# Pooled attention and a squared-ReLU network: pooling by accumulating transfers, a longer lag of the second product, and SyncE's transfers in another order

## The chip, the cores and the metric

The kernel runs on one core of one Trainium2 chip. The metric is the device time of one execution in microseconds (us). Engines are called as the profile calls them: PE (matrix product; PEld is its loading of weights), DVE (vector), ACT (scalar), POOL (GpSimd), SP (SyncE, which issues transfers), and a "q" behind a name means the engine's instruction queue. Differences of about 0.5% are the least that runs of this kernel can tell from nothing.

## The reference, cut to what matters

```python
def _attn_ref(q, k, v):                        # each 8 x 8 x 576 x 64: batch, head, token, width
    k_p = k.reshape(B, H, 72, 8, D).mean(axis=3)   # every 8 tokens of keys become one
    v_p = v.reshape(B, H, 72, 8, D).mean(axis=3)
    scores = scale * np.matmul(q, k_p.transpose(0, 1, 3, 2))
    scores = scores - np.max(scores, axis=-1, keepdims=True)
    attn = np.exp(scores)
    attn = attn / (np.sum(attn, axis=-1, keepdims=True) + 1e-09)
    return np.matmul(attn, v_p)

x = attn_out.transpose(0, 2, 1, 3).reshape(4608, 512)
h = np.maximum(x @ w_in, 0.0)                  # w_in 512 x 2048
return h * h @ w_out                           # w_out 2048 x 512
```

The two weights come as 64-bit floats and are turned into 32-bit floats on the chip.

## The kernel before, in words

The 4608 tokens go through in nine chunks of 512 (`CH`, numbered 0 to 8). A chunk has 16 steps, one for each block `fc` of 128 hidden units, so there are 144 steps; the loop over them is at line 734. In step s, PE makes the first product (x times w_in, tile `h`) of step s, and then the second product (squared ReLU times w_out, tiles `o`, function `project`) of step s - LAG, with LAG = 2. What the attention needs is woven into the same steps.

**The first product.** From chunk 2 on the function `seven` makes two blocks `fc` at once with seven products in place of eight: 24 matmuls in an even step, 18 in an odd one, each 128x256. Sums of quarters of x and of the weights (`x_sums`, `x_operand`; `sum_of_quarters`) feed it, and DVE and ACT add the parts up in PSUM (tiles `u` and `h`: `soon` in the even step). In the odd step, `activate` makes r = relu(h) and its square on ACT, for both blocks.

**High and low parts.** Products at nearly full precision are made of three: each operand is split into a rounded high part and what is left. ACT copies the high part, DVE subtracts: `gh` and `gl` from r (`split_hidden`, line 564), `x_B`/`x_T` from sums of x, `st` from q, `kh`/`kl` from pooled keys. `project` is 12 matmuls of 128x512 in a step: for each of four `o` tiles two with `gh` and one with `gl`.

**w_out.** Its 16 blocks, split, are kept in device memory (`kept`), and each block is fetched again for each chunk (`fetch_weights`, line 200): a transfer of 512 KB, issued from ACT's queue, one step ahead of its use (STREAM = 1). It lands in one of the 39 slots of 4 KB per partition that all large tiles share (`w_tile`, SLOTS).

**Keys and values.** Those of batches 0 and 1 are pooled at the start, by additions on POOL. From batch 2 on, `kv_steps` (line 702) plans, for each of the 8 heads, a load of 72 rows of 8 x 64 numbers (`load_head`, 144 KB, from SP) and two steps later one reduction on DVE (`pool_head`, line 243): tiles `kq` for keys, `vp` for values. The table KV_AT holds the steps, counted from KV0 = -37 before the chunk that first needs the batch: k in the steps 0 to 9, PE's transposition `turn_k` (tile `kps`) in step 13, v in the steps 18 to 31. Six batches (2 to 7) go this way, one for each of the chunks 2 to 7.

**Attention of a chunk.** For each of four pairs of heads, from chunk 2 on, eight stages follow at the distances in `STEADY` from the steps -23, -19, -15 and -11 before the chunk: q is loaded (two steps ahead, QL) and transposed on DVE; `scores` on PE (tiles `sps`), then a maximum over partitions on POOL (tile `mx`, PARTITION_ALL_REDUCE); `exponents` two steps later, with a sum over partitions on POOL (`tot`); `send_sums` and `fetch_sums` carry the sums through device memory (`rs`, `rc`) to another layout, `reciprocals` works on them on DVE (`rr`) and sends them (`rd`), `fetch_reciprocals` spreads them over partitions (`rb`); `weigh_values` is PE's product with the values (`av`), which DVE multiplies by `rb` into `xf`. Chunks 0 and 1 have stages of their own (`token_...`).

**What sets the order.** No scheduler moves anything: the class `InOrder` (line 26) keeps every instruction, on its engine, in the order in which the loop writes it down, and each engine works strictly in that order. A tile tag with `bufs` buffers makes an instruction wait until the tile that lay there has been read. SP, ACT's queue and POOL are such orders too: a transfer that waits holds up all transfers behind it.

Of the kernel before, what the change touches and what calls it, by code (L numbers as in the profile page):

```python
# [9 lines left out]
F32 = mybir.dt.float32  # L10
# [27 lines left out]
def pooled_attn_relu2_ffn(  # L38
# [42 lines left out]


    STEADY = ((-23, -19, -15, -11), (0, 1, 3, 5, 5, 6, 6, 8))
    KV0 = -37
    EARLY = ((-16, -13, -10, -8), (0, 1, 2, 3, 4))
    KV_AT = ((0, 1, 2, 3, 4, 5, 8, 9), 13, (18, 19, 22, 23, 26, 27, 30, 31))
# [15 lines left out]
    def load(dst, src):  # L102
        loads.append((dst, src))
# [77 lines left out]
    def sum_of_quarters(g, name):  # L181
        (e, kh), a, b, op = {"S1": ((1, 1), (1, 0), (1, 1), ALU.add), "S3": ((1, 0), (0, 0), (1, 0), ALU.subtract),
                             "S2": ((1, 1), (1, 1), (0, 0), ALU.subtract), "S4": ((0, 1), (0, 1), (1, 1), ALU.subtract)}[name]
        t = quarter(g, e, kh)
        DVE.tensor_tensor(t, quarter(g, *a), quarter(g, *b), op=op)
        split_operand(g, name, t)

    stored = {}

# [23 lines left out]
    def load_head(kind, b, h):  # L213
        t = loaded[kind, b, h] = sb.tile([SP_, POOL * D], F32, name=f"{kind}_{b}_{h}", tag="ld", bufs=LD)
        load(t, {"k": k, "v": v}[kind][b, h].rearrange("(s o) d -> s (o d)", o=POOL))

    def load_pair(kind, b, p):
        t = loaded[kind, b, p] = w_tile(F32, f"{kind}8_{b}_{p}")[:SP_]
# [8 lines left out]
        GP.tensor_tensor(dst, src[:, :, :D], src[:, :, D:2 * D], op=ALU.add)  # L227

    def halve_k(b, p):
        kp = loaded["kp", b, p] = sb.tile([SP_, 2, D], F32, name=f"kq_{b}_{p}", tag="kq", bufs=4)  # L230
        by_halves(kp, loaded.pop(("k", b, p)))

    def halve_v(b, p):
# [6 lines left out]
        for i in range(2):  # L240
            DVE.tensor_reduce(kv[b][:, 2 * p + i, :], t[:, i].rearrange("p (o d) -> p d o", d=D), axis=AX.X, op=ALU.add)

    def pool_head(kind, b, h):
        new_batch(b)
        if kind == "v":
            dst = kv[b][:, h, :]
        else:
            if h % 2 == 0:
                loaded["kp", b, h // 2] = sb.tile([SP_, 2, D], F32, name=f"kq_{b}_{h // 2}", tag="kq", bufs=4)
            dst = loaded["kp", b, h // 2][:, h % 2, :]  # L250
        DVE.tensor_reduce(dst, loaded.pop((kind, b, h)).rearrange("p (o d) -> p d o", d=D), axis=AX.X, op=ALU.add)

    def turn_k(b, pairs=range(NPAIR)):

# [84 lines left out]
        return then  # L339

    def reduced(kind, c, p):
        return [sb.tile([SP_, CH], F32, name=f"{kind}_{c}_{p}_{i}", tag="mx", bufs=4) for i in range(2)]

    def exponents(c, p):
        sc, mx = live.pop((c, p))
# [96 lines left out]

    def weigh_values(c, p):

        if c >= PLAIN and p == 0:
            xf[c] = sb.tile([P, NPAIR, CH], F32, name=f"xf_{c}", tag="xf", bufs=1)
        sc, rb = live.pop((c, p))
        av = (ps_a if c else ps_h).tile([P, 512], F32, name=f"av_{c}_{p}", tag="a" if c else "h")
        for b, o, n in segments(c):
            for i in range(2):  # L450
                PE.matmul(av[i * D:(i + 1) * D, o:o + n], lhsT=kv[b][:, 2 * p + i, :], rhs=sc[:, i, o:o + n],
                          start=True, stop=True)

        def then():
            if c == 0:
                x = xts[c, p] = x_tile(F32, f"x_{c}_{p}")
                ACT.copy(x[:, 0, :], av)
            elif c < PLAIN:
                x = xts[c, p] = x_tile(F32R, f"x_{c}_{p}")
                split(x[:, 0, :], x[:, 1, :], av)  # L460
            else:
                DVE.tensor_tensor(xf[c][:, p, :], av, rb, op=ALU.mult)

        return then

# [1 line left out]

    def x_sums(c):

        one, two = (xf[c][:, i:i + 2, :].rearrange("p c (h t) -> p h c t", h=2) for i in (0, 2))  # L470
# [4 lines left out]
    minus = {"T2": "T1", "T4": "T2"}  # L475

    def x_operand(c, name):
        src = xf[c][:, :2, :HT] if name == "B11" else parts[name]
# [65 lines left out]
    def hidden(c, fc):  # L544
        if c < PLAIN:
            hps = [(fc, plain(c, fc))]
        else:
            hps = seven(c, fc)
            if fc % 2 == 0:
                return hps  # L550

        def activate():
            for f, hp in hps:
                if c == 0:
                    r = gts[c, f] = sb.tile([P, CH], F32, name=f"r_{c}_{f}", tag="gl" if f % 2 else "gh", bufs=2)
                else:
                    r = gts[c, f] = sb.tile([P, CH], F32, name=f"r_{c}_{f}", tag="r", bufs=2)
                ACT.activation(r, hp, AF.Relu)
            for f, _ in hps:
                ACT.activation(gts[c, f], gts[c, f], AF.Square)  # L560

        return (activate, None, None) if c >= PLAIN else (None, None, activate)

    def split_hidden(c, fc):
        if c == 0:
            return
        gh = sb.tile([P, CH], F32R, name=f"gh_{c}_{fc}", tag="gh", bufs=2)
# [109 lines left out]
        halve_k(1, p)  # L677
    for p in range(NPAIR):
        halve_v(1, p)
    at(0, turn_k, 1)  # L680
    at(9, split_k, 1)


# [16 lines left out]
            at(c * NFC + i + LAG - STREAM, fetch_weights, c, i)  # L700

    def kv_steps(b, s):
        k_at, turn_at, v_at = KV_AT
        for h in range(H):
            at(s + k_at[h], load_head, "k", b, h)
            at(s + k_at[h] + 2, pool_head, "k", b, h)
            at(s + v_at[h], load_head, "v", b, h)
            at(s + v_at[h] + 2, pool_head, "v", b, h)
        at(s + turn_at, turn_k, b)
# [90 lines left out]
```

## Time and profile before

| what | value |
|---|---|
| median of 3 runs | 1018.83 us (1016.66 to 1021.34) |
| profiled execution | 1017.44 us |
| its span, first to last instruction | 1015.5 us, so 1.94 us lie around it |
| mean granted clock of PE | 0.978 |
| PE busy | 937.0 us (92%) |
| DVE busy | 651.0 us (64%) |
| ACT busy | 513.6 us (51%) |
| POOL busy | 335.1 us (33%) |

A page of the profile lists, for each engine, the busy time and groups of instructions: output tile <- input tiles, the shape, how many (x), busy us in all, mean ns of one, and how long the engine stood idle just before them, with who ended it. The view of windows gives the same by stretches of time, the view of waits who waited for whom, and the timeline single instructions. Matmuls overlap, so a PE that reads as busy can still be slowed down; how far apart they start tells more.

### The profile page before, as it was taken

The numbers are of one execution on the slowest core, as the hardware profiler recorded it, in microseconds if no ns is written. First come the engines' busy times: TensorE is split into PE (matmuls) and PEld (weight loads), VectorE is DVE, ScalarE is ACT, GpSimd is POOL, SyncE is SP. The second block draws the span as 40 slices with busy tenths as digits, with TensorE's granted clock in tenths as the row PEclk, the third lists the DMA queues.
The fourth block names the chain that finished last, engine by engine and source line by source line (L and its number), as shares of the span: only waits on it lengthen the run. The fifth ranks groups of instructions, "written<-read, shape, count | busy, mean of one in ns | idle before, by whom it ended". The sixth has DMA issues, their size and how long they took to land.

```text
span 1015.5 us, 14298 instructions
## 1 busy us (share of the span) xinstructions
PE 937.0 (92%) x5050; PEld 728.1 (72%) x5050; DVE 651.0 (64%) x1043; ACT 513.6 (51%) x1015; POOL 335.1 (33%) x162
## 2 busy tenths in 40 slices
PE   5789999998988989999999998999999999999997
PEld 3334444576866777787878786878788878888996
DVE  4877288867577777866686658665856675434231
ACT  2565476555555454644455535544554465435333
POOL 6720013443415434343444432433344434300000
PEclk9989999999999999999999899999999999999999
DMA  9667404475433433543445344543344434223223
GB/s 222 189 164 238 135 0 138 154 252 189 152 86 132 124 116 109 170 143 111 122 140 169 117 123 119 169 122 117 116 157 117 114 107 160 95 105 135 103 104 125
DMA packets 133686, 138.65 MB, mean 137 GB/s; under 512 B 91576, under 2 KB 91576, under 8 KB 133616
## 3 DMA queue, kind: packets, MB, share of 16 engines
q1 hardware_dynamic: 115184, 70.63, 24.6%
q10 hardware_dynamic: 18432, 67.12, 19.3%
q8 instruction: 40, 0.66, 0.3%
q14 instruction: 30, 0.25, 0.1%
HBM read 119.65 MB, written 18.06 MB: 136 GB/s over the span
## 4 chain that ended last, share of the span: by engine, by line
PE 54%; DVE 23%; ACT 9%; DMA 7%; issue 4%; SPq 2%; POOL 1%; ACTq 0%; DVEq 0%; POOLq 0%
PE o L34 26%; PE h L34 24%; DVE gl L34 4%; DMA w_o<-kept 4%; DVE h L34 3%; DVE vp L34 2%; SPq L34 2%; PE sps L34 2%; DVE xf L34 2%; DVE kq L34 2%; ACT sc L34 2%; PE av L34 2%; DMA k<-in_k_dram 1%; DVE sc L34 1%; DVE st L34 1%
## 5 line engine op out<-in xcount | busy, mean ns | idle before, releaser
L34 PE MATMUL o<-w_o,gh 128*128 128x512 f32 x1024 | 331.5, 405 | 23.0 <-ACT gh L34 15.1
L34 POOL PARTITION_ALL_REDUCE tot<-sc x56 | 183.0, 3315 | 327.6 <-ACT sc L34 238.2
L34 PEld LDWEIGHTS o<-w_o,gh 128*128 128x128 f32 x1024 | 188.5, 193 | 71.8 <-ACT gh L34 23.2
L34 PE MATMUL o<-w_o,gl 128*128 128x512 f32 x512 | 209.1, 408 | 18.6 <-DVE gl L34 17.6
L34 POOL PARTITION_ALL_REDUCE mx<-sc x56 | 111.9, 2046 | 207.1 <-ACT sc L34 177.9
L34 DVE TENSOR_TENSOR gl<-r,gh 128x512 fp32r<-128x512 f32 x128 | 114.6, 895 | 93.5 <-ACT gh L34 92.7
L34 ACT ACTIVATE r<-h 128x512 f32<-128x512 f32 x144 | 85.8, 596 | 111.7 <-PE h L34 71.3
L34 PEld LDWEIGHTS o<-w_o,gl 128*128 128x128 f32 x512 | 98.5, 192 | 57.4 <-DVE gl L34 37.1
L34 PE MATMUL h<-x_T,w_S 128*128 128x256 f32 x1008 | 131.4, 284 | 2.2 <-DVE x_T L34 1.4
L34 PEld LDWEIGHTS h<-x_T,w_S 128*128 128x128 f32 x1008 | 125.1, 192 | 3.8 <-DVE x_T L34 2.2
L34 ACT COPY u<-h 128x256 f32<-128x256 f32 x112 | 41.8, 373 | 131.3 <-DVE h L34 67.1
L34 DVE TENSOR_TENSOR h<-h,u 128x256 f32<-128x256 f32 x168 | 72.6, 432 | 50.9 <-ACT u L34 26.8
L34 PE MATMUL h<-x_B,w_A 128*128 128x256 f32 x672 | 99.4, 284 | 0.0
L34 PEld LDWEIGHTS h<-x_B,w_A 128*128 128x128 f32 x672 | 93.4, 193 | 4.8
L34 ACT ACTIVATE r<-r 128x512 f32<-128x512 f32 x144 | 84.2, 625 | 1.0
L34 ACT CAST gh<-r 128x512 fp32r<-128x512 f32 x128 | 78.5, 613 | 1.6 <-PE o L34 0.4
L34 ACT ACTIVATE sc<-sc 72x512 f32<-72x512 f32 x56 | 34.5, 632 | 68.3 <-DVE sc L34 68.3
L34 PE MATMUL o<-wf_o,r 128*128 128x512 f32 x128 | 61.6, 627 | 0.0
L34 PE MATMUL h<-x,wf_i 128*128 128x512 f32 x128 | 61.4, 625 | 0.0
L34 DVE TENSOR_TENSOR st<-qs,st 64x512 fp32r<-64x512 f32 x56 | 42.1, 751 | 27.1 <-ACT st L34 26.3
L34 DVE TENSOR_TENSOR u<-h,u 128x256 f32<-128x256 f32 x56 | 23.6, 421 | 53.9 <-ACT u L34 53.4
L34 DVE TENSOR_REDUCE kq<-k 72x64 f32<-72x512 f32 x48 | 50.7, 1060 | 7.1 <-PE kps L34 6.2
(85 smaller groups left out, 1179.3 us busy)
## 6 DMA issues: line engine op xcount, KB each, us to landing
w_o<-kept ACTq DMA_DIRECT2D x128, 512.0 KB
out_dram<-ob SPq DMA_DIRECT2D x36, 256.0 KB
raw_i<-in_moe_w_in_dram SPq DMA_DIRECT2D x16, 512.0 KB
raw_o<-in_moe_w_out_dram SPq DMA_DIRECT2D x16, 512.0 KB
kept<-w_o SPq DMA_DIRECT2D x16, 512.0 KB
rb<-rd SPq DMA_DIRECT2D x56, 128.0 KB
k<-in_k_dram SPq DMA_DIRECT2D x48, 144.0 KB
v<-in_v_dram SPq DMA_DIRECT2D x48, 144.0 KB
```

The lines of the kernel that those rows point to most:

```text
L34: return lambda *a, **k: self.tc.keep_in_program_order(f(*a, **k))
```

## The change

1. **Pooling.** `load_head` and `pool_head` go. `load_sums` brings the keys of a batch as four rounds of [72 partitions, 8 heads, 2 x 64 numbers]: round 0 is a plain load from SP, and the rounds 1 to 3 are added onto it in the same tile by transfers that accumulate, issued from POOL, two (four heads each) for a round. `pool` then makes one addition on DVE of the two halves, for all 8 heads. The same for values. The tile `two` has one buffer, so each of these steps waits for the one before it.
2. **Steps of it.** KV_AT becomes (k from step 3, v from step 9), KV0 becomes -34: for keys, rounds in the steps 3 to 6, the addition in 8, `turn_k` in 9; for values, rounds in 9 to 12, the addition in 14.
3. **The lag.** LAG becomes 3: `project` in step s is for step s - 3. `split_hidden` stays at s - 2, so `gh` and `gl` are written a step before they are used; they get three buffers each.
4. **Subtractions held back.** The DVE half of a split goes on a list `behind` and is written down by `catch_up`: in odd steps before `soon`, in all steps after PE's part.
5. **SP.** `fetch_weights` moves from ACT's queue to SP's, to the start of a step (still one step ahead of use). `fetch_sums` and `fetch_reciprocals` come next, ahead of the loads, one step later than before (`STEADY` (0, 1, 3, 5, 5, 6, 6, 8) becomes (0, 1, 3, 5, 6, 6, 7, 8)); `x_sums` moves to the end of a step.
6. **Room.** SLOTS 40 for 39; `xf` becomes two of these slots; tag `ld` two buffers for three, `mx` three for four, `kq` one of eight heads for four of two.

On PE, the rows below are the end of the first product in an odd step and the start of the second product behind it, in chunk 2 (`h_10`, `h_11` are the blocks of the step pair; the digit behind `w_o`, `gh` and `gl` is the block `fc` that is projected). Before:

```order
L34 MATMUL h_10_3006<-x_B_2210,w_S_2795 128x256 x6
L34 MATMUL h_10_3006<-x_B_2283,w_A_1653 128x256 x6
L34 MATMUL h_11_3007<-x_T_2287,w_A_1773 128x256 x6
L34 MATMUL o_0_2478<-w_o_9_3073,gh_9_3104 128x512 x2
L34 MATMUL o_0_2478<-w_o_9_3073,gl_9_3105 128x512
```

The same place now:

```order
L34 MATMUL h_10_2911<-x_B_2131,w_S_2738 128x256 x6
L34 MATMUL h_10_2911<-x_B_2198,w_A_1592 128x256 x6
L34 MATMUL h_11_2912<-x_T_2202,w_A_1731 128x256 x6
L34 MATMUL o_0_2447<-w_o_8_2949,gh_8_2951 128x512 x2
L34 MATMUL o_0_2447<-w_o_8_2949,gl_8_2952 128x512
```

Behind the same products of block 11 stands block 8 of the second product, where block 9 stood.

On POOL, the rows below run from the sums of one pair of heads to the maxima of the next chunk's first pair (ISA rows with `mx` are maxima, with `tot` sums; the digit behind them is the pair). Before:

```order
L34 ISA mx_2_0_2499<-sc_2_2498 72x512
L34 ISA mx_2_1_2500<-sc_2_2498 72x512
L34 ISA tot_2_0_2642<-sc_2_2498 72x512
L34 ISA tot_2_1_2643<-sc_2_2498 72x512
L34 ISA mx_3_0_2776<-sc_3_2775 72x512
L34 ISA mx_3_1_2777<-sc_3_2775 72x512
L34 ISA tot_3_0_2935<-sc_3_2775 72x512
L34 ISA tot_3_1_2936<-sc_3_2775 72x512
L34 ISA mx_0_0_3065<-sc_0_3064 72x512
L34 ISA mx_0_1_3066<-sc_0_3064 72x512
L34 ISA tot_0_0_3203<-sc_0_3064 72x512
```

The same place now, with batch 4's keys and values:

```order
L34 ISA mx_2_0_2396<-sc_2_2395 72x512
L34 ISA mx_2_1_2397<-sc_2_2395 72x512
L34 DMA k_4_2326<-in_k_dram 72x4x128 x6
L34 ISA tot_2_0_2554<-sc_2_2395 72x512
L34 ISA tot_2_1_2555<-sc_2_2395 72x512
L34 ISA mx_3_0_2680<-sc_3_2679 72x512
L34 ISA mx_3_1_2681<-sc_3_2679 72x512
L34 DMA v_4_2760<-in_v_dram 72x4x128 x2
L34 ISA tot_3_0_2842<-sc_3_2679 72x512
L34 ISA tot_3_1_2843<-sc_3_2679 72x512
L34 DMA v_4_2760<-in_v_dram 72x4x128 x2
L34 ISA mx_0_0_2971<-sc_0_2970 72x512
```

Six accumulating transfers (three rounds) stand between the maxima and the sums of pair 2; the rounds for values stand one by one between later reductions, the third behind the rows shown.

The diff, cut to its core:

```diff
-    LAG, QL = 2, 2
+    LAG, QL = 3, 2
-    SLOTS, STREAM, LD = 39, 1, 3
+    SLOTS, STREAM, LD = 40, 1, 2
-    STEADY = ((-23, -19, -15, -11), (0, 1, 3, 5, 5, 6, 6, 8))
-    KV0 = -37
+    STEADY = ((-23, -19, -15, -11), (0, 1, 3, 5, 6, 6, 7, 8))
+    KV0 = -34
...
+    behind = []
+
+    def catch_up():
+        while behind:
+            behind.pop(0)()
+
     def split_operand(g, name, src):
         t = wt[g, name] = w_tile(F32R, f"w_{g}_{name}")
-        split(in_blocks(t[:, 0, :]), in_blocks(t[:, 1, :]), src)
+        hi, lo = in_blocks(t[:, 0, :]), in_blocks(t[:, 1, :])
+        ACT.copy(hi, src)
+        behind.append(lambda: DVE.tensor_tensor(lo, src, hi.bitcast(F32), op=ALU.subtract))
...
     def fetch_weights(c, fc):
         t = wt["o", fc] = w_tile(F32R, f"w_o_{c}_{fc}")
-        ACT.dma_start(t.bitcast(F32), stored[fc])
+        dma(t.bitcast(F32), stored[fc])
...
-    def pool_head(kind, b, h):
-        new_batch(b)
+    two = {}
+
+    def load_sums(kind, b, j):
+
+        if j == 0:
+            new_batch(b)
+            two[kind] = sb.tile([SP_, H, 2 * D], F32, name=f"{kind}2_{b}", tag="two", bufs=1)
+        src = {"k": k, "v": v}[kind][b].rearrange("h (s j o) d -> j s h (o d)", j=POOL // 2, o=2)[j]
+        if j == 0:
+            load(two[kind], src)
+        else:
+            for n in range(0, H, H // 2):
+                GP.dma_start(two[kind][:, n:n + H // 2], src[:, n:n + H // 2], accum_op=ALU.add)
+
+    def pool(kind, b):
+        t = two.pop(kind)
...
-        DVE.tensor_reduce(dst, loaded.pop((kind, b, h)).rearrange("p (o d) -> p d o", d=D), axis=AX.X, op=ALU.add)
+        DVE.tensor_tensor(dst, t[:, :, :D], t[:, :, D:], op=ALU.add)
...
-        gh = sb.tile([P, CH], F32R, name=f"gh_{c}_{fc}", tag="gh", bufs=2)
-        gl = sb.tile([P, CH], F32R, name=f"gl_{c}_{fc}", tag="gl", bufs=2)
-        split(gh, gl, gts[c, fc])
+        gh = sb.tile([P, CH], F32R, name=f"gh_{c}_{fc}", tag="gh", bufs=3)
+        gl = sb.tile([P, CH], F32R, name=f"gl_{c}_{fc}", tag="gl", bufs=3)
+        r = gts[c, fc]
         gts[c, fc] = (gh, gl)
+        ACT.copy(gh, r)
+        behind.append(lambda: DVE.tensor_tensor(gl, r, gh.bitcast(F32), op=ALU.subtract))
...
+        for kind, start in KV_AT:
+            for j in range(POOL // 2):
+                at(s + start + j, load_sums, kind, b, j)
+            at(s + start + POOL // 2 + 1, pool, kind, b)
+        at(s + KV_AT[0][1] + POOL // 2 + 2, turn_k, b)
...
-        if 0 <= s - LAG < len(steps):
-            split_hidden(*steps[s - LAG])
+        for f, a in todo:
+            if f is fetch_weights:
+                f(*a)
+        if 0 <= s - 2 < len(steps):
+            split_hidden(*steps[s - 2])
         if store:
             store()
         store = project(*steps[s - LAG]) if s >= LAG else None
+        if s % 2:
+            catch_up()
         if soon:
             soon()
         for f in later:
             f()
         if then:
             then()
+        catch_up()
+        first = (load_q, load_sums)
         for f, a in todo:
-            if f is fetch_weights:
+            if f in (fetch_sums, fetch_reciprocals):
+                f(*a)
+        for f, a in todo:
+            if f in first:
                 f(*a)
         issue_loads()
         for f, a in todo:
-            if f is not fetch_weights and f not in on_pe + last + (x_operand,):
+            if f not in first + on_pe + last + (x_sums, x_operand, fetch_weights, fetch_sums, fetch_reciprocals):
                 f(*a)
```

More of the change, by code (lines that the diff above doesn't have):

```diff
@@ L71, in pooled_attn_relu2_ffn @@
     SCALE = 1.0 / (D ** 0.5) / POOL
[L72 removed]
+    LAG, QL = 3, 2
     PLAIN = 2
     SQ = 32
[L76 removed]
+    SLOTS, STREAM, LD = 40, 1, 2
     FIRST, EAGER, AHEAD = 2, 8, 3
     PRO, RATE, MARGIN = 5, 2, 1
[L83 to L86 removed]
+    STEADY = ((-23, -19, -15, -11), (0, 1, 3, 5, 6, 6, 7, 8))
+    KV0 = -34
+    EARLY = ((-15, -12, -10, -7), (0, 1, 2, 3, 4))
+    KV_AT = (("k", 3), ("v", 9))
     X_AT = (("B11", -9), ("B22", -2), ("T1", -2), ("T3", -2), ("T2", -1), ("B21", -1), ("T4", -1))
@@ L185, in sum_of_quarters @@
         DVE.tensor_tensor(t, quarter(g, *a), quarter(g, *b), op=op)
-        split_operand(g, name, t)
+        behind.append(lambda: split_operand(g, name, t))
     stored = {}
@@ L211, in pooled_attn_relu2_ffn @@
     heads = [(i, slice(i * D, (i + 1) * D), slice((1 - i) * D, (2 - i) * D)) for i in range(2)]
-    def load_head(kind, b, h):
-        t = loaded[kind, b, h] = sb.tile([SP_, POOL * D], F32, name=f"{kind}_{b}_{h}", tag="ld", bufs=LD)
-        load(t, {"k": k, "v": v}[kind][b, h].rearrange("(s o) d -> s (o d)", o=POOL))
     def load_pair(kind, b, p):
@@ L229, in halve_k @@
     def halve_k(b, p):
-        kp = loaded["kp", b, p] = sb.tile([SP_, 2, D], F32, name=f"kq_{b}_{p}", tag="kq", bufs=4)
+        if p == 0:
+            loaded["kq", b] = sb.tile([SP_, H, D], F32, name=f"kq_{b}", tag="kq", bufs=1)
+        kp = loaded["kp", b, p] = loaded["kq", b][:, 2 * p:2 * p + 2, :]
         by_halves(kp, loaded.pop(("k", b, p)))
@@ L241, in reduce_v @@
             DVE.tensor_reduce(kv[b][:, 2 * p + i, :], t[:, i].rearrange("p (o d) -> p d o", d=D), axis=AX.X, op=ALU.add)
-    def pool_head(kind, b, h):
-        new_batch(b)
+    two = {}
[11 more added lines that the diff above has]
+        t = two.pop(kind)
         if kind == "v":
-            dst = kv[b][:, h, :]
+            dst = kv[b]
         else:
-            if h % 2 == 0:
-                loaded["kp", b, h // 2] = sb.tile([SP_, 2, D], F32, name=f"kq_{b}_{h // 2}", tag="kq", bufs=4)
-            dst = loaded["kp", b, h // 2][:, h % 2, :]
-        DVE.tensor_reduce(dst, loaded.pop((kind, b, h)).rearrange("p (o d) -> p d o", d=D), axis=AX.X, op=ALU.add)
+            dst = sb.tile([SP_, H, D], F32, name=f"kq_{b}", tag="kq", bufs=1)
+            for p in range(NPAIR):
+                loaded["kp", b, p] = dst[:, 2 * p:2 * p + 2, :]
+        DVE.tensor_tensor(dst, t[:, :, :D], t[:, :, D:], op=ALU.add)
     def turn_k(b, pairs=range(NPAIR)):
@@ L341, in reduced @@
     def reduced(kind, c, p):
-        return [sb.tile([SP_, CH], F32, name=f"{kind}_{c}_{p}_{i}", tag="mx", bufs=4) for i in range(2)]
+        return [sb.tile([SP_, CH], F32, name=f"{kind}_{c}_{p}_{i}", tag="mx", bufs=3) for i in range(2)]
     def exponents(c, p):
@@ L443, in weigh_values @@
     def weigh_values(c, p):
-        if c >= PLAIN and p == 0:
-            xf[c] = sb.tile([P, NPAIR, CH], F32, name=f"xf_{c}", tag="xf", bufs=1)
+        if c >= PLAIN and p % 2 == 0:
+            xf[c, p // 2] = w_tile(F32, f"xf_{c}_{p // 2}")
         sc, rb = live.pop((c, p))
@@ L461, in then @@
             else:
-                DVE.tensor_tensor(xf[c][:, p, :], av, rb, op=ALU.mult)
+                DVE.tensor_tensor(xf[c, p // 2][:, p % 2, :], av, rb, op=ALU.mult)
         return then
@@ L468, in x_sums @@
     def x_sums(c):
-        one, two = (xf[c][:, i:i + 2, :].rearrange("p c (h t) -> p h c t", h=2) for i in (0, 2))
+        one, two = (xf[c, i].rearrange("p c (h t) -> p h c t", h=2) for i in range(2))
         parts.update({"B11": one[:, 0], "B21": two[:, 0], "B22": two[:, 1], "T1": one[:, 0], "T3": one[:, 1], "T2": two[:, 1], "T4": two[:, 0]})
@@ L477, in x_operand @@
     def x_operand(c, name):
-        src = xf[c][:, :2, :HT] if name == "B11" else parts[name]
+        src = xf[c, 0][:, :, :HT] if name == "B11" else parts[name]
         if name in minus:
@@ L554, in activate @@
                 if c == 0:
-                    r = gts[c, f] = sb.tile([P, CH], F32, name=f"r_{c}_{f}", tag="gl" if f % 2 else "gh", bufs=2)
+                    r = gts[c, f] = sb.tile([P, CH], F32, name=f"r_{c}_{f}", tag="gl" if f % 2 else "gh", bufs=3)
                 else:
@@ L679, in pooled_attn_relu2_ffn @@
         halve_v(1, p)
-    at(0, turn_k, 1)
+    at(1, turn_k, 1)
     at(9, split_k, 1)
@@ L702, in kv_steps @@
     def kv_steps(b, s):
[L703 to L709, printed above, removed]
+        for kind, start in KV_AT:
[3 more added lines that the diff above has]
+        at(s + KV_AT[0][1] + POOL // 2 + 2, turn_k, b)
     ready = {0, 1}
@@ L764, in pooled_attn_relu2_ffn @@
             activate()
-        for kind in (x_operand, sum_of_quarters):
+        for kind in (x_sums, x_operand, sum_of_quarters):
             for f, a in todo:
```

## Prediction

> **What bounds the kernel now.** I first cut the span into windows at the first copy of each chunk's output (`ob`), to see which stretch pays. Columns: busy us and count of each engine, granted clock of PE, share of the transfer engines.
>
> ```profile
> core 0: us, PE busy (x) PEld busy (x) DVE busy (x) ACT busy (x) POOL busy (x), PEclk, DMA share, GB/s
> 202.00:320.00 118.00, 105.05 (x495) 81.72 (x493) 82.72 (x117) 62.77 (x117) 42.38 (x16) 0.96 0.50 159
> 320.00:428.00 108.00, 97.58 (x576) 80.63 (x577) 81.99 (x128) 57.54 (x113) 42.75 (x16) 0.98 0.43 130
> 428.00:532.00 104.00, 97.58 (x591) 82.72 (x591) 72.92 (x111) 52.32 (x103) 41.99 (x16) 0.98 0.44 133
> 532.00:638.00 106.00, 99.81 (x602) 84.64 (x601) 73.82 (x113) 53.60 (x105) 42.97 (x17) 0.97 0.44 134
> 638.00:742.00 104.00, 98.58 (x602) 84.53 (x602) 70.36 (x109) 53.62 (x106) 42.03 (x17) 0.97 0.42 128
> 742.00:839.00 97.00, 94.97 (x579) 80.33 (x578) 61.92 (x97) 51.00 (x100) 40.28 (x16) 1.00 0.43 128
> 839.00:929.00 90.00, 88.78 (x537) 76.70 (x537) 42.73 (x76) 43.50 (x85) 20.44 (x9) 1.00 0.34 113
> ```
>
> These are chunks 1 to 7, their ends rounded to whole us. The first six take 118 + 108 + 104 + 106 + 104 + 97 = 637 us. Chunk 7 has the same products, no pooling, and half of the next attention: 90 us, at full clock. No engine but PE is near full, so the first six are PE plus waits.
>
> What PE needs alone I take from the chain of waits where it ran on PE unbroken, and the product with the values from the timeline (start, us, piece):
>
> ```profile
> 429.66 0.94 PE sps L34 x8
> 430.59 2.73 PE o L34 x12
> 433.32 2.15 PE h L34 x18
> 435.47 2.75 PE o L34 x12
> 438.22 2.89 PE h L34 x24
> ...
> 474.56 4.01 PE o L34 x10
> ```
>
> ```profile
> 470.31 1.08 PE L34 MATMUL av<-sc,vp 72*64 72x256 f32 x8
> ```
>
> Two steps are 2.15 + 2.89 + 2 x 2.75 = 10.54 us, so 16 steps are 84.3, and with four pairs' `sps` and `av`, 4 x (0.94 + 1.08) = 8.1, a full chunk is 92.4. Chunk 7, with about half of the 8.1, should take 88.3 and takes 90: 1.7 us of loss. Chunk 3 (428 to 532) loses 11.6.
>
> Who makes PE wait in the six chunks (view of waits: us in all, times, longest):
>
> ```profile
> PE o L34 <- DVE gl L34: 17.6, 25, 1.6
> PE o L34 <- ACT gh L34: 15.1, 14, 2.8
> PE o L34 <- DMA w_o<-kept: 3.8, 6, 1.2
> PE sps L34 <- DVE st L34: 2.3, 5, 0.5
> PE h L34 <- DVE x_T L34: 1.4, 4, 0.3
> ```
>
> The timeline shows how one comes about (in brackets the idle time before, and who ended it):
>
> ```profile
> 470.22 1.28 DVE L34 TENSOR_TENSOR sc<-sc,mx 72x512 f32<-72x512 f32 x2
> ...
> 470.93 1.23 ACT L34 ACTIVATE sc<-sc 72x512 f32<-72x512 f32 x2 [3.55 <-DVE sc L34]
> ...
> 472.07 0.60 ACT L34 CAST gh<-r 128x512 fp32r<-128x512 f32 x1
> ...
> 472.70 1.80 DVE L34 TENSOR_TENSOR gl<-r,gh 128x512 fp32r<-128x512 f32 x1 [1.20 <-ACT gh L34]
> ...
> 472.73 0.73 PE L34 MATMUL o<-w_o,gh 128*128 128x512 f32 x2 [1.33 <-ACT gh L34]
> ...
> 474.56 0.50 PE L34 MATMUL o<-w_o,gl 128*128 128x512 f32 x1 [1.10 <-DVE gl L34]
> ```
>
> DVE comes late to `sc`, ACT stands 3.55 us before it, `gh` and `gl` stand behind, and PE needs both in this same step. Then the next 10 matmuls take 4.01 us where 12 took 2.73: the clock has dropped.
>
> **Part by part.** *The lag.* `gh` and `gl` are made in step s - 2 of their block as before, but PE reads them a step later: 10.54 / 2 = 5.3 us more, against longest waits of 2.8 and 1.6. Both rows go: 17.6 + 15.1 = 32.7 us. The drops of the clock follow such stalls; by the windows they cost 0.04 x 118 + 0.02 x 108 + 0.02 x 104 + 0.03 x 106 + 0.02 x 104 = 14.2 us, and I let them go with the stalls (bounds 0 and 14.2; at 742 to 839, with few waits, the clock is 1.00).
>
> What is late next is r. It has two buffers and ACT may not overwrite it before `gl` has read it. The view of waits and the page:
>
> ```profile
> ACT r L34 <- DVE gl L34: 36.6, 29, 1.7
> ```
>
> ```profile
> L34 ACT ACTIVATE r<-h 128x512 f32<-128x512 f32 x144 | 85.8, 596 | 111.7 <-PE h L34 71.3
> ```
>
> PE now covers this, since it waits for `gl` itself. Then only its 2.75 us of `o` matmuls lie between `h` of one step and the next; two relus of 0.6 leave 1.55. The longest wait overshoots by 0.15, so at most 29 x 0.15 = 4.4 us come back. I take all 4.4.
>
> *DVE's reductions.* They go, and 12 additions of 72x512 come (the nearest row is `sc`):
>
> ```profile
> L34 DVE TENSOR_REDUCE kq<-k 72x64 f32<-72x512 f32 x48 | 50.7, 1060 | 7.1 <-PE kps L34 6.2
> L34 DVE TENSOR_REDUCE vp<-v 72x64 f32<-72x512 f32 x50 | 52.8, 1058 | 0.0
> L34 DVE TENSOR_TENSOR sc<-sc,mx 72x512 f32<-72x512 f32 x56 | 35.8, 680 | 0.0
> ```
>
> 96 x 1.06 - 12 x 0.68 = 94 us of DVE, some 15 us of every chunk. DVE is not the bound, so none of it is a term by itself: it is why I let both rows above go in full, and it shortens the two other waits on DVE, 2.3 + 1.4 = 3.7; I take half, 1.9 (bounds 0 and 3.7).
>
> *POOL's rounds.* No POOL transfer is in this trace. The groups of instructions nearest to one are POOL's addition over the same loaded keys and its reductions; ACT's copy stands ahead of them:
>
> ```profile
> L34 POOL PARTITION_ALL_REDUCE mx<-sc x56 | 111.9, 2046 | 207.1 <-ACT sc L34 177.9
> ...
> L34 ACT COPY sc<-sps 72x512 f32<-72x512 f32 x56 | 30.4, 584 | 21.0 <-PE sps L34 20.4
> ...
> L34 POOL TENSOR_TENSOR k<-k 72x512 f32<-72x512 f32 x8 | 10.5, 1314 | 13.3 <-DMA q<-in_q_dram 7.4 <-DMA k<-in_k_dram 5.9
> ```
>
> By tile, with min, median and max in ns:
>
> ```profile
> L34 POOL PARTITION_ALL_REDUCE tot<-sc x56: 3232/3310/4487, 164.2 to 882.5; - x56
> ```
>
> ```profile
> L34 DVE TENSOR_TENSOR xf<-xf x28: 640/692/2692, 279.6 to 919.5; 128x512 f32<-128x512 f32 x28
> ```
>
> Of transfers there are SP's issue of a load of 144 KB (timeline), 512 KB that the chain waits for, and SP's waits for 2 KB to land and for POOL:
>
> ```profile
> 507.85 0.30 SPq L34 DMA_DIRECT2D k<-in_k_dram  x1
> ```
>
> ```profile
> 500.81 3.12 DMA w_o<-kept
> ```
>
> ```profile
> SPq L34 <- POOL tot L34: 105.4, 24, 11.2
> ...
> SPq L34 <- DMA rs<-tot: 38.4, 30, 4.3
> ```
>
> A round is two issues on POOL and one landing, since the next round waits for it. Lower end: 2 x 0.30 + 38.4 / 30 = 1.9 us. Upper end: 2 x 3.3 (POOL's longest kind) + 4.3 = 10.9. I take POOL's addition over as many bytes and `w_o`'s landing, 2 x 1.31 + 3.12 = 5.7: four times the bytes, but in whole rows and without an addition.
>
> Three rounds for keys stand between `mx` and `tot` of pair 2. Behind `tot` stands SP's `rs`, and behind that the fetch of `w_o` for the step after next. Counted from the start of the step that has pair 2's scores, with 92.4 / 16 = 5.8 us a step: `mx` is done after about 9.1 (`h` 2.9, `sps` 0.9, two copies 1.2, two reductions 4.1); then come three rounds of R each, `tot` 6.6, two issues 0.6, a landing 3.1. PE needs that `w_o` six steps and one `h` later, at 6 x 5.8 + 2.5 = 37.3. So R may be (37.3 - 9.1 - 6.6 - 0.6 - 3.1) / 3 = 6.0 us. With 5.7 the rounds cost nothing; the keys' addition on DVE and PE's `kps` are due later still. Beyond 6.0 each us costs 3 x 6 batches = 18 us. The rounds for values stand singly where POOL idles.
>
> *`w_o` on SP's queue.* A fetch may now stand behind an SP wait for POOL, 105.4 / 24 = 4.4 us; from its place it has 5.8 + 2.2 = 8.0, which leaves 3.6 against 3.12 to land: nothing. The longest, 11.2, would cost 11.2 + 3.1 - 8.0 = 6.3; once for each of six batches that is 38. The other end is the 3.8 us of `w_o` waits above, gone. I take 0. Loads of q stay two steps ahead, `rc` and `rb` move a step with their users, fewer buffers of `mx` lengthen POOL's wait for `rs` inside the 9.1: no term.
>
> The sum, on the profiled execution: 1017.4 - 32.7 - 14.2 - 1.9 + 4.4 = 973.0. The median shown stands 1018.83 - 1017.44 = 1.4 higher, so 974.4.
>
> **A rule against the change.** DVE's additions get as long as 2.69 us (`xf`, median 0.69), and I see this beside POOL's reductions, while `tot` reaches only 4.5 for 3.3. The Trainium skill, "SBUF — State Buffer" ("SBUF: two separate sides" and the section on the bandwidth pool), says that DVE and GpSimd lock one pair of ports against each other, that a transfer issued from GpSimd waits with its descriptors while DVE holds it, and that one of 620 ns then took 3100. The rows agree that the two stretch each other, mostly DVE; for a POOL transfer no row can. An estimate by that page of the Trainium skill, 2 x 2.5 us more in a round, gives 10.7 and a total of 974.4 + 4.7 x 18 = 1059.
>
> **The rivals.** *The waits move.* PE no longer stops for `gl`, but ACT does before r, and `h` stops for r. If every us came back there, clock and all, only the 1.9 would stay: about 1016.9. For it: ACT's 36.6. Against it: the longest of those is 1.7, and DVE gets 15 us lighter per chunk.
>
> *POOL's rounds become the bound: slower.* Place: three rounds ahead of `tot` of pair 2, then `rs`, then `w_o`. It starts at 6.0 us a round, eats the whole gain at 6.0 + 44.4 / 18 = 8.5, and is slower by over 0.5% from 8.8. At the upper end, 10.9, it is 974.4 + 4.9 x 18 = 1063. For it: POOL's own instructions of 3.3 us, and that its transfers may be held up as above. Against it: the nearest rows give 5.7.
>
> *PE's floor is reached.* Chunk 1 needs 16 x 2 x 2.75 + 8.1 = 96.1, the next five 92.4 each, together 558; with chunk 7's loss of 1.7 in each, 568.2 for 637: 68.8 less, 950. That is the low end of the forecast's case, not another sign.
>
> **How the numbers follow.** The forecast's mechanism, with its floor, has 0.72: its waits and the move are in the rows. The waits that move have 0.11, the rounds 0.17, since their price is the one that no row shows. A run of this kernel can tell about 0.5%, 5 us, from nothing: 1013.7 to 1023.9 is "same". So faster is 0.72, same 0.11, slower 0.17. The range goes from the floor, 950, through the second case to 1024, and leaves out the third.
>
> **What would show it.** Right: no `o` matmul waits for `gh` or `gl`; the clock stays at 1.00 between 300 and 700; chunks 2 to 6 take 93 to 98 us; the six accumulating transfers before `tot` take under 18 us. Wrong: `h` waiting for r; `o` waiting for `w_o` behind `rs`; `kps` or the keys' addition waiting for a POOL transfer; POOL busy from one `mx` to the next.

## The result, and the profile after

| | median | ratio to before, 95% interval |
|---|---|---|
| before | 1019.61 us (4 runs) | |
| after | 1050.76 us (4 runs, 1048.47 to 1054.12) | 1.031 [1.027, 1.035] |

The change makes the kernel 3% slower. The prediction was 974.4 us and faster.

First the stretches, as windows of the profile after, now cut at that kernel's own first copies of `ob` for chunks 1, 3 and 6 (length, busy us and count of each engine, granted clock, share of the transfer engines):

```profile
core 0: us, PE busy (x) PEld busy (x) DVE busy (x) ACT busy (x) POOL busy (x), PEclk, DMA share, GB/s
209.80:333.00 123.20, 104.10 (x484) 81.97 (x483) 67.04 (x103) 60.65 (x114) 57.69 (x29) 0.93 0.55 148
...
443.70:558.90 115.20, 98.52 (x597) 85.88 (x596) 55.38 (x99) 52.66 (x105) 56.00 (x29) 0.93 0.50 122
...
789.20:882.50 93.30, 93.30 (x578) 81.03 (x577) 54.43 (x92) 50.98 (x101) 41.23 (x17) 1.00 0.40 126
```

Chunk 1 took 118 us before and takes 123.2 now, chunk 3 took 104 and takes 115.2. Chunk 6, which has none of POOL's rounds (17 instructions on POOL for 29), fell from 97 to 93.3 and runs without a stall: its PE column equals its length. So the loss lies where the rounds are.

The view of waits of the kernel after (us in all, times, longest) says who stops PE there:

```profile
PE h L34 <- ACT r L34: 35.8, 6, 8.6
PE kps L34 <- DVE kq L34: 27.3, 5, 6.9
...
PE o L34 <- DMA w_o<-kept: 8.1, 8, 3.8
```

The 17.6 us for `gl` and 15.1 us for `gh` are gone, as forecast. In their place stand five waits of `kps` for the keys' addition and six of `h` for r, about one of each for a batch. Both are among the signs of being wrong that the prediction names. `w_o`, the place where I had expected trouble, is small.

POOL's timeline over the keys of one batch (start, us, instruction, in brackets the idle time before and who ended it):

```profile
442.58 3.96 POOL L34 PARTITION_ALL_REDUCE mx<-sc  x2 [1.79 <-ACT sc L34]
446.42 1.25 POOL L34 DMA_DIRECT2D k<-in_k_dram  x1
451.25 1.21 POOL L34 DMA_DIRECT2D k<-in_k_dram  x1 [3.58 <-issue]
455.75 1.19 POOL L34 DMA_DIRECT2D k<-in_k_dram  x1 [3.28 <-issue]
462.20 1.20 POOL L34 DMA_DIRECT2D k<-in_k_dram  x1 [5.27 <-issue]
466.38 1.19 POOL L34 DMA_DIRECT2D k<-in_k_dram  x1 [2.98 <-issue]
470.37 1.19 POOL L34 DMA_DIRECT2D k<-in_k_dram  x1 [2.79 <-ACT r L34]
471.12 7.53 POOL L34 PARTITION_ALL_REDUCE tot<-sc  x2
```

The six transfers take 471.12 - 446.42 = 24.7 us, 8.2 a round, where I had 5.7 and wrote "under 18 us". The two transfers of one round do not depend on each other, yet the second of each (451.25, 462.20, 470.37) comes 4 to 6.5 us behind the first. "Issue" means that the trace shows nothing the instruction waited for. The median time from the start of such an issue to its landing is 4.1 us on the page, so the second starts about when the first has landed. The landings of the single transfers in the trace say it more closely: each of the five behind the first starts 0.3 us after the one before it has landed (450.93 and 451.25, 455.43 and 455.75, and so on; the last too, though its row names ACT). From the start of one round to the next it is 9.3 and 10.6 us; the mean of the three is 8.2 because POOL does not stay for the landing of the last.

What the long rounds do to the others, from the timeline of the same kernel, at the keys' addition and at the values':

```profile
474.27 0.69 DVE L34 TENSOR_TENSOR kq<-k 72x512 f32<-72x512 f32 x1 [6.80 <-DMA k<-in_k_dram]
475.10 0.71 PE L34 MATMUL kps<-ident,kq 72*128 72x72 f32 x4 [4.76 <-DVE kq L34]
...
523.61 0.69 DVE L34 TENSOR_TENSOR vp<-v 72x512 f32<-72x512 f32 x1 [11.43 <-DMA v<-in_v_dram]
524.93 1.23 ACT L34 ACTIVATE sc<-sc 72x512 f32<-72x512 f32 x2 [13.81 <-DVE sc L34]
526.07 0.60 ACT L34 CAST gh<-r 128x512 fp32r<-128x512 f32 x1
526.58 0.58 ACT L34 ACTIVATE r<-h 128x512 f32<-128x512 f32 x1
527.22 1.65 PE L34 MATMUL h<-x_B,w_A 128*128 128x256 f32 x6 [8.58 <-ACT r L34]
```

DVE works strictly in order, so its addition `vp` holds up the next `sc` for 11.43 us; ACT's exponents wait for that, `gh` and the next relu stand behind them, and the PSUM tile of `h` is not free until the relu has read it. PE stops for 8.58 us. With the 4.76 us at `kps` that is 13.3 us for this batch.

Chunk 3 takes 115.2 us here and 97.8 in the run with double room below, 17.4 less. What the two stops leave open lies right behind them: in the windows from 475.10 to 479.70 and from 527.20 to 530.90 PE is busy throughout (8.3 us) at a granted clock of 0.50. An estimate from this half speed is 4.1 us, and 13.3 + 4.1 = 17.4.

### The profile page after: what moved, and what is told of

It reads as the page before. It is cut to its first block, busy times and chain, and to the rows that moved or that the text cites. A ratio compares the mean times of both kernels' runs of the same rounds, so it can differ in the third digit from the quotient of the medians.

```text
span 1052.3 us, 14125 instructions
## 1 busy us (share of the span) xinstructions
PE 938.6 (89%) x5050; PEld 740.4 (70%) x5050; DVE 555.3 (53%) x959; ACT 509.4 (48%) x1015; POOL 421.0 (40%) x234
## 3 DMA queue, kind: packets, MB, share of 16 engines
q0 software_dynamic: 28800, 10.68, 8.8%
## 5 line engine op out<-in xcount | busy, mean ns | idle before, releaser
L34 POOL PARTITION_ALL_REDUCE tot<-sc x56 | 191.9, 3474 | 178.0 <-issue 153.4
L34 PEld LDWEIGHTS o<-w_o,gh 128*128 128x128 f32 x1024 | 189.6, 194 | 54.8 <-issue 13.3
L34 PE MATMUL o<-w_o,gl 128*128 128x512 f32 x512 | 203.4, 397 | 0.0
L34 PE MATMUL h<-x_T,w_S 128*128 128x256 f32 x1008 | 136.7, 290 | 3.3 <-DVE x_T L34 1.7
L34 POOL PARTITION_ALL_REDUCE mx<-sc x56 | 108.4, 1982 | 64.4 <-ACT sc L34 63.2
L34 PEld LDWEIGHTS h<-x_T,w_S 128*128 128x128 f32 x1008 | 130.2, 199 | 5.3 <-DVE x_T L34 2.9
L34 DVE TENSOR_TENSOR gl<-r,gh 128x512 fp32r<-128x512 f32 x128 | 108.1, 858 | 34.6 <-ACT gh L34 34.6
L34 PEld LDWEIGHTS o<-w_o,gl 128*128 128x128 f32 x512 | 98.6, 193 | 22.3
L34 POOL DMA_DIRECT2D k<-in_k_dram x36 | 43.7, 1214 | 125.2 <-issue 119.3
L34 POOL DMA_DIRECT2D v<-in_v_dram x36 | 44.2, 1227 | 120.1 <-issue 62.9
L34 PE MATMUL o<-wf_o,r 128*128 128x512 f32 x128 | 65.1, 656 | 0.0
L34 DVE TENSOR_TENSOR st<-qs,st 64x512 fp32r<-64x512 f32 x56 | 46.9, 837 | 25.1 <-ACT st L34 24.3
```

What stands on the lines that cost most here:

```text
L34: return lambda *a, **k: self.tc.keep_in_program_order(f(*a, **k))
```

## The experiments

The theory (A): a round of accumulating transfers is long because POOL can't issue the second transfer while the first fills the room for descriptors (`dynamic_dma_scratch_size`, 1024 bytes of each partition here), and the long rounds are the whole loss. Rivals: another part of the change costs the time; accumulating is slow in itself; or the loss is a matter of where the additions stand. The kernel before took 1018.12, 1016.82 and 1017.88 us beside the three groups of runs, so each ratio is against its own neighbour.

**The change without the new pooling** (the loads and reductions by heads of before, with their table and start; tag `ld` with four buffers; LAG 3, SP's order and the rest as after; the diff is cut):

```diff
-    KV_AT = (("k", 3), ("v", 9))
+    KV_AT = ((0, 1, 2, 3, 4, 5, 8, 9), 13, (18, 19, 22, 23, 26, 27, 30, 31))
...
-            at(s + start + POOL // 2 + 1, pool, kind, b)
+            at(s + k_at[h] + 2, pool_head, "k", b, h)
```

> The changed kernel with the old pooling: heads loaded one by one from SP and reduced on DVE, at the old steps (the ld tag has four buffers, two of them in the room of the tile that is gone). Theory A (the accumulating rounds on POOL make DVE's additions late, and all else of the change is a gain): 970 to 985 us, no o matmul waits for gh or gl, no kps wait for DVE. Theory B (the lag and SP's order cost time themselves, since r and w_o become late): 1010 us or more, with h waiting for ACT r and o for w_o.

Measured: 988.14 us, ratio 0.971 [0.968, 0.974]; somewhat above the range. Its waits:

```profile
PE h L34 <- ACT x_T L34: 15.5, 4, 4.8
...
PE sps L34 <- DVE st L34: 8.6, 6, 3.7
```

No wait for `gl` or `gh` is left, so the lag does what I said. But 42.5 us were forecast for it (32.7 + 14.2 - 4.4), and 30.0 came (1018.12 - 988.14): `h` waits elsewhere for 15.5 us, and by the windows the clock stays at 0.97 to 0.98 in chunks 1 to 4. The run holds the rest of the change as well, the move of `w_o`, the new order within a step and small moves of the stages of chunks 0 and 1 (`EARLY`) among it, so the lag's own share is not shown.

**The new pooling alone** (the kernel before with `load_sums` and `pool`, LAG 2):

> The kernel before with the new pooling alone (its steps, its tiles, mx with three buffers, ld with two); lag 2, w_o on ACT's queue and the order on SP stay. Theory A: worse than the changed kernel, 1060 to 1100 us, since the late additions on DVE meet a second product that has no step to spare. Theory B: 1000 to 1020 us, since DVE only gets lighter.

Measured: 1087.03 us, ratio 1.068 [1.064, 1.073], as A has it.

```profile
PE o L34 <- ACT gh L34: 55.3, 12, 12.6
PE kps L34 <- DVE kq L34: 23.3, 5, 6.8
```

The new pooling costs 69 us here. With a lag of two the wait for the values shows up at `gh`: in the timeline five of the 12 waits, 7.0 to 12.6 us each, end 3 to 5 us behind an addition `vp` that had waited for its transfer. The pooling is the loss, and the rest of the change covers a part of it.

**Double room for descriptors** (the third buffer of `gl` makes the space):

```diff
-        gl = sb.tile([P, CH], F32R, name=f"gl_{c}_{fc}", tag="gl", bufs=3)
+        gl = sb.tile([P, CH], F32R, name=f"gl_{c}_{fc}", tag="gl", bufs=2)
...
-    nc = _bacc.Bacc("TRN2", target_bir_lowering=False, num_devices=1, dynamic_dma_scratch_size=1024)
+    nc = _bacc.Bacc("TRN2", target_bir_lowering=False, num_devices=1, dynamic_dma_scratch_size=2048)
```

> The changed kernel with 2048 bytes per partition for the descriptors of POOL's transfers where it had 1024 (gl has two buffers for three, to make room). Theory A with its cause in that room (a transfer fills over half of it, so that the second of a round is only written when the first has landed): the two transfers of a round overlap, a round takes 5 to 6.5 us for 9.2, and the time falls to 985 to 1005 us. If the transfers of a round follow one another for another reason: rounds of 9 us and 1045 to 1055 us.

Measured: 976.60 us, ratio 0.960 [0.956, 0.964], 74.2 below after and better than I expected. POOL's timeline over the same six transfers:

```profile
519.13 2.50 POOL L34 DMA_DIRECT2D k<-in_k_dram  x2
524.26 1.19 POOL L34 DMA_DIRECT2D k<-in_k_dram  x1 [2.64 <-DMA k<-in_k_dram]
525.97 1.18 POOL L34 DMA_DIRECT2D k<-in_k_dram  x1 [0.51 <-DMA k<-in_k_dram]
530.27 1.20 POOL L34 DMA_DIRECT2D k<-in_k_dram  x1 [3.13 <-DMA k<-in_k_dram]
532.80 1.19 POOL L34 DMA_DIRECT2D k<-in_k_dram  x1 [1.32 <-ACT r L34]
533.55 7.02 POOL L34 PARTITION_ALL_REDUCE tot<-sc  x2
```

Both transfers of the first round go back to back, and three rounds take 14.4 us, 4.8 a round (5.1 and 6.0 from the start of one to the next). None of these transfers waits for "issue" any more, only for the landing that the sum itself requires: each of the last four starts 0.4 us after the transfer with the same heads has landed, the last too (landing at 532.40), though its row names ACT. What is left on PE's side of the two kinds of wait that mattered:

```profile
PE o L34 <- DMA w_o<-kept: 4.0, 4, 2.2
PE h L34 <- ACT r L34: 3.7, 8, 1.2
```

The long waits of `kps` for `kq` and of `h` for r are gone.

**Two buffers of `gl` alone**, to see that the room did it and not the buffer:

> Only the third buffer of gl is taken away; the room for POOL's descriptors stays as in the changed kernel. Theory A (the room made the gain of the kernel with double room, the buffer had no part in it): 1045 to 1060 us, POOL still issues the second transfer of a round only after the first has landed. Rival B (the buffer changed the order of waits and made the gain): below 1000 us.

Measured: 1051.51 us, ratio 1.036 [1.032, 1.039]. The buffer had no part.

**The additions two steps later** (single room):

```diff
-    KV_AT = (("k", 3), ("v", 9))
+    KV_AT = (("k", 3), ("v", 11))
...
-            at(s + start + POOL // 2 + 1, pool, kind, b)
-        at(s + KV_AT[0][1] + POOL // 2 + 2, turn_k, b)
+            at(s + start + POOL // 2 + 3, pool, kind, b)
+        at(s + KV_AT[0][1] + POOL // 2 + 4, turn_k, b)
```

> The changed kernel with DVE's addition and turn_k two steps later, and the values' rounds two steps later with them. Theory A with the additions as its place: DVE finds the rounds landed, the waits of kps for kq and of h for r go, 985 to 1005 us. Theory C (the place is the one that the prediction named, tot behind the rounds, then rs, then w_o): still 1035 us or more, with o waiting for w_o.

Measured: 1063.02 us, ratio 1.043 [1.038, 1.049]. This missed what I expected of my own theory, and fits C, the place that the prediction had named.

```profile
PE h L34 <- ACT x_T L34: 48.0, 5, 10.9
PE o L34 <- DMA w_o<-kept: 35.2, 6, 7.9
```

With DVE's waits out of the way, `kps` and r no longer stop PE, but that place's wait comes, `o` for `w_o`, six times, once a batch, and with it a larger one that it had not named, `h` for x's operands. By its timeline, three rounds of values now stand between a pair's maxima and sums as well (500.27 to 527.62 us). The long rounds hit whichever user is due first, and moving one exposes the next.

**The same move with double room:**

> The kernel with double room (976.6 us), with the additions on DVE and the transposition two steps later and the rounds for values from step 11. With single room the same move took 1063. Theory A (the long rounds were the root, and both places, DVE's additions and the sums behind the rounds, were only where they showed): 972 to 985. Rival B (the move itself is bad, since the values' rounds then stand together ahead of the sums): 990 or more.

Measured: 978.90 us, ratio 0.962 [0.959, 0.964]. With short rounds the move costs nothing that can be told; in single room it cost 12 us. The places were symptoms.

**Transfers that don't accumulate** (single room):

```diff
-                GP.dma_start(two[kind][:, n:n + H // 2], src[:, n:n + H // 2], accum_op=ALU.add)
+                GP.dma_start(two[kind][:, n:n + H // 2], src[:, n:n + H // 2])
```

> POOL's transfers overwrite in place of accumulating; they have the same number, size and order, and the room stays single. What is left out is the sum: the pooled keys and values of batches 2 to 7 are those of the last round. Theory A (the room for descriptors makes a round long, whatever the transfer does): the second transfer is still issued only after the first has landed, a round stays at 8 to 9.5 us, and the time at 1035 to 1055. Rival B (accumulating makes it long): a round falls to 5 to 6 us and the time below 1000.

Measured: 967.71 us, ratio 0.953 [0.949, 0.957]: outside A's range and inside B's. So theory A fell in the form I had given it: in the same room, transfers of the same size do go back to back. (In the third round the second one starts 0.4 us after the half that it overwrites has landed, at 522.72.) Its timeline, then the queue of POOL's transfers on its page (packets, MB, share of the transfer engines) and POOL's groups:

```profile
513.04 1.47 POOL L34 DMA_DIRECT2D k<-in_k_dram  x2
517.21 1.42 POOL L34 DMA_DIRECT2D k<-in_k_dram  x2 [2.71 <-DMA k<-in_k_dram]
521.04 0.71 POOL L34 DMA_DIRECT2D k<-in_k_dram  x1 [2.41 <-DMA k<-in_k_dram]
523.11 0.72 POOL L34 DMA_DIRECT2D k<-in_k_dram  x1 [1.36 <-ACT sc L34]
```

```profile
q0 software_dynamic: 4608, 10.65, 4.0%
...
L34 POOL DMA_DIRECT2D k<-in_k_dram x36 | 26.2, 730 | 45.2 <-DMA k<-in_k_dram 38.1 <-DMA w_o<-kept 2.8 <-ACT r L34 2.6
```

The same rows of the page after:

```profile
q0 software_dynamic: 28800, 10.68, 8.8%
...
L34 POOL DMA_DIRECT2D k<-in_k_dram x36 | 43.7, 1214 | 125.2 <-issue 119.3
```

For the same bytes, an accumulating transfer is 28800 / 72 = 400 packets, a plain one 4608 / 72 = 64, and it takes POOL 1.21 us to issue for 0.73. The amended theory: the room is counted in packets, and 400 fill it so far that another 400 do not fit.

**A round in four transfers of two heads** (single room):

```diff
-            for n in range(0, H, H // 2):
-                GP.dma_start(two[kind][:, n:n + H // 2], src[:, n:n + H // 2], accum_op=ALU.add)
+            for n in range(0, H, H // 4):
+                GP.dma_start(two[kind][:, n:n + H // 4], src[:, n:n + H // 4], accum_op=ALU.add)
```

> The room is single, and a round is four accumulating transfers of two heads in place of two of four heads: the same bytes and about the same packets, half of them in a transfer. Theory A (what waits is room for packets: one transfer of 400 fits, two don't, but two of 200 do): two transfers of a round are issued back to back, the others as those before them land, a round is 6.5 to 8.5 us and the time 1010 to 1045. Rival B (in single room POOL can have only one accumulating transfer under way, of whatever size): four landings one behind the other, a round over 10 us, the time above 1060. Rival C (the packets' own 64 ns are the limit, whatever the division): 1045 to 1056.

Measured: 1046.70 us, ratio 1.028 [1.025, 1.032], just above A's range, within that of C. The timeline of POOL shows which:

```profile
445.75 2.36 POOL L34 DMA_DIRECT2D k<-in_k_dram  x2
450.87 2.31 POOL L34 DMA_DIRECT2D k<-in_k_dram  x2 [2.76 <-issue]
454.39 1.15 POOL L34 DMA_DIRECT2D k<-in_k_dram  x1 [1.22 <-issue]
...
471.30 6.93 POOL L34 PARTITION_ALL_REDUCE tot<-sc  x2
```

Two go back to back and the third waits for "issue", which is the amended theory: by its page (29952 packets for 144 transfers, 208 each) 416 fit and 624 don't. B is out. But the round is still 25.55 / 3 = 8.5 us. What counts is the packets that may be under way at once, about 400, and these take about as long to land in two pieces as in one. That the packets' own time sets the round (C) is out as well: with double room the same packets take 4.8 us a round, though in both traces a packet of 512 bytes takes a median of 65 ns.

**Three times the room**, and **three times the room with a round in one transfer of eight heads**:

> Two buffers of gl and three times the room. Theory A (double room already holds both transfers of a round, and the next round waits for their landing, so more room changes nothing): 972 to 981. Rival B (transfers are still held up by room at double room): below 970.

> Three times the room, and a round is one accumulating transfer of all 8 heads. Theory A (POOL's part of a round is about 1.2 us for each half, and most of it is for the packets): POOL's issue takes 2 to 2.5 us, a round stays at 5 us, the time within 5 us of the kernel with three times the room and two transfers. Rival B (the issue costs the same whatever its size): 1.2 us an issue, a round 1.2 us shorter, the time 5 to 10 us lower. Rival C (one large transfer lands later, since nothing starts before all of it is written down): slower by over 5 us.

Measured: 976.34 us, ratio 0.960 [0.957, 0.962], and 983.37 us, 0.966 [0.963, 0.969]. More room than two transfers need brings nothing, as A has it. For the undivided transfer A and B are wrong and C is right in the time, slower by 7.0; that nothing starts before all of it is written down is not shown. POOL's issue takes only 1.4 us for twice the bytes, but the transfer lands a median of 7.4 us after it, and the rounds wait for landings (timeline of POOL, undivided):

```profile
523.58 1.46 POOL L34 DMA_DIRECT2D k<-in_k_dram  x1
530.29 1.40 POOL L34 DMA_DIRECT2D k<-in_k_dram  x1 [5.25 <-DMA k<-in_k_dram]
542.17 1.39 POOL L34 DMA_DIRECT2D k<-in_k_dram  x1 [10.48 <-DMA k<-in_k_dram]
543.02 6.97 POOL L34 PARTITION_ALL_REDUCE tot<-sc  x2
```

Three rounds here take 19.4 us, 6.5 each.

**`w_o` on ACT's queue again**, in the kernel with double room (the fetch keeps its new place at the start of a step):

> The kernel with double room and two buffers of gl (976.6 us), but w_o is fetched from ACT's queue as before the change. Theory A (the move to SP's queue is worth about nothing): 973 to 981. Rival B (SP's queue keeps w_o off ACT, whose issues delay gh and r): 985 or more. Rival C (SP's waits for POOL hold w_o up): below 972, with PE's 4.0 us of waits for w_o gone.

Measured: 985.18 us, ratio 0.972 [0.968, 0.975]; 8.6 us above, which is B. The group of `gh` on ACT in this kernel, and after it the same group in the kernel with `w_o` on SP's queue:

```profile
L34 ACT CAST gh<-r 128x512 fp32r<-128x512 f32 x128 | 78.7, 615 | 37.5 <-PE o L34 27.8 <-PE h L34 6.7 <-DMA rc<-rs 2.1
```

```profile
L34 ACT CAST gh<-r 128x512 fp32r<-128x512 f32 x128 | 78.6, 614 | 1.0 <-PE o L34 0.4
```

In the timeline of the first of them the fetch stands right ahead of a `gh` that waits:

```profile
432.97 0.33 ACTq L34 DMA_DIRECT2D w_o<-kept  x1
433.34 0.62 ACT L34 CAST gh<-r 128x512 fp32r<-128x512 f32 x1 [1.49 <-PE o L34]
```

The same `gh`, with the same buffers, doesn't wait for `o` in the other kernel. The fetch does, since its slot must have been read by `o` first, and so ACT's copies stand behind a transfer's wait. On SP's queue nothing of ACT stands behind it.

Two things stay open. PE waits for `gh` in neither kernel; by the view of waits it is `sps` that waits longer for `st`, 22.3 us for 12.0, in a profiled execution that is the slowest of its six, and how the late copies lead there is not shown. And this is the worth of the queue with the fetch at the start of a step. In the kernel before, the fetch was on ACT's queue too but later in the step, and ACT hardly stood still ahead of `gh`:

```profile
L34 ACT CAST gh<-r 128x512 fp32r<-128x512 f32 x128 | 78.5, 613 | 1.6 <-PE o L34 0.4
```

So 8.6 us is not shown to be what the move as a whole was worth.

**The new pooling alone, with double room** (the kernel before, LAG 2; one of the 39 slots makes the space):

> The kernel before with the new pooling alone (LAG 2), and double room for POOL's descriptors, for which one of the 39 slots goes. With single room it took 1087. Theory A (with short rounds the pooling relieves DVE and so part of the waits for gl and gh): 1000 to 1015, o waits for gl and gh together 15 to 28 us. Rival B (the lag was what made the pooling bearable): above 1018. Rival C (the pooling was the whole gain, and the lag adds nothing to it): below 985.

Measured: 1022.86 us, ratio 1.007 [1.003, 1.010], above A's range and with B. With lag 2, `o` still waits 21.2 us for `gh`, 9.8 for `gl` and 15.9 for `w_o` by the view of waits, against 15.1, 17.6 and 6.5 before. Those for `gh` and `gl` together hardly fell, so the work that left DVE is not the limit there. That those for `w_o` grew may be the rounds or the slot that was given away; no run tells which. Beside short rounds the rest of the change brings 46.3 us (1022.86 - 976.60), beside the old pooling 30.0: each gains more with the other.

## Why the prediction was wrong, point by point

- **The failed step is the price of a round.** "I take POOL's addition over as many bytes and `w_o`'s landing, 2 x 1.31 + 3.12 = 5.7". The two issues are 1.2 us each, near that. The step's model was what failed, "two issues on POOL and one landing": with single room the second issue waits for the first landing, so that a round is two landings one behind the other, 8.2 us in the mean. The room for descriptors was no term at all. With double room the model holds: 4.8 us.
- **The place.** "[...] the keys' addition on DVE and PE's `kps` are due later still. [...] The rounds for values stand singly where POOL idles." By my own rule, 18 us for each us above 6.0, 8.2 would have cost 40 us, at `w_o`. It cost 74 (1050.76 - 976.60), 63.1 of it as stops at the two additions on DVE (27.3 + 35.8). Nor was `kps` due later: `mx` starts 5.0 us into the step by my count and at 442.58 in the trace, and PE stood at `kps` from 470.34, which makes 32.8 against the 37.3 of `w_o`. I gave the values' rounds no due time at all, though their addition stands on DVE ahead of `sc`. The `w_o` chain is real: it took over when the additions moved. So the rival "POOL's rounds become the bound" had the sign and the cause, but not the place, and by its price 8.2 us a round would have left the kernel at about 1014, still no slower than before.
- **The lag.** Right in mechanism: both rows of 17.6 and 15.1 went. Of 42.5 us forecast with the clock and r, 30.0 came, in a run that has the rest of the change too; most of what is missing is the clock (below). The 4.4 for r was near: with double room `h` waits 3.7 for r.
- **DVE's reductions.** With double room the new pooling brings 988.14 - 976.60 = 11.5 us beside the lag; I had 1.9. The 15.5 us that `h` waits for x's operands without it are gone there. Beside LAG 2 no gain shows (1022.86, with a slot less).
- **`w_o` on SP's queue.** I took 0, between a gain of 3.8 and a loss of 38. In the kernel with double room the queue alone, at the new place in the step, is a gain of 8.6; the move from the old place was not measured. I asked what SP's queue would do to `w_o`, and not what ACT's queue had `w_o` do to `gh` once the order within a step changed.
- **The sum.** With the rounds at 4.8 us the kernel takes 976.6 us against 974.4 forecast, but as -30.0 and -11.5 for -42.5 and -1.9: near by errors that cancel, which is luck.
- **The clock as a term.** I priced its drops at 14.2 us from the windows and let them go with the waits. They are stretches at a granted clock of 0.50, by windows set to them 30.6 us in chunks 1 to 6 before, 23.8 in the run without the new pooling, 74.8 after and 6.8 with double room. At half speed 30.6 us cost an estimated 15.3, so the price was near, but with the lag alone only some 3 of it went. The level between the drops is another matter. In the kernel with double room the windows show 0.95 from chunk 2 on:

```profile
419.00:516.80 97.80, 94.81 (x597) 82.66 (x597) 57.84 (x99) 52.49 (x105) 55.30 (x29) 0.95 0.61 144
711.20:804.60 93.40, 93.40 (x578) 81.08 (x577) 54.15 (x93) 51.02 (x101) 40.02 (x17) 0.95 0.43 125
```

Chunk 6 takes 93.4 us there at 0.95 and 93.3 us at 1.00 in the kernel after. So that column times a length is no price by itself; the stretches at half are.
- **The rule on ports.** The estimate by the Trainium skill, "SBUF — State Buffer" ("SBUF: two separate sides" and the section on the bandwidth pool), was 10.7 us a round and 1059 us, not far from what came, and that is luck. The cause it gives is not what the runs show: with double room DVE is as busy (563.5 us for 555.3) and POOL's issues are no shorter (1.33 us for 1.21), and yet a round is 4.8 us.

## What to carry to other kernels

Two transfers that don't depend on each other can still run one behind the other: before counting them as "two issues and one landing", ask how many packets each has and how many the queue can hold, and find out with a run that changes only that room. When a transfer is made longer, list every instruction in order behind its landing on each engine and give each a due time; the earliest one is the bound, and moving that one only shows the next. Where a transfer that waits for a buffer stands in the queue of an engine that also computes, look at what stands right behind it: at the start of a step it held up ACT's copies, later in the step it did not.

## What the runs showed of the hardware that was not expected

- An accumulating transfer of 144 KB from POOL is 400 packets and 1.2 us of POOL's time, a plain one 64 packets and 0.73 us.
- With 1024 bytes of each partition for descriptors, 416 packets of POOL's transfers could be under way and 624 could not; with 2048, 800 could. A POOL that lacks room stands still, and all its reductions with it; the trace calls it "issue" (119.3 us ahead of the transfers of keys). The word alone doesn't tell of a lack of room: with double room 207.9 us of "issue" still stand ahead of `tot`. The Trainium skill, "DMA: Bandwidth & Descriptors" (Terms), says that descriptors of transfers issued this way are written to rings in SBUF, which agrees with a room that is paid for in SBUF.
- Time from issue to landing of accumulating transfers grew with the packets: for the keys, by the pages, a median of 4.1 us for 400 alone, 6.0 where two of these are under way, 7.4 for one of 28224 / 36 = 784. A plain one of 64 packets took 4.3 with two under way.
- The best version of these runs that keeps the sums is the change with double room or more, 976.60 and 976.34 us, 4% faster than before; the kernel with plain transfers, which leaves them out, is 8.9 us below the first, about what accumulating still costs.
